# Two attentions in one kernel: raw loads parked in the second one's weight place, and the first 512 rows' five tiles grown together

## The chip, the core and the metric

One core of one Trainium2 chip runs the kernel. The metric is the device time of one execution in microseconds (us); less is better. TensorE does the matmuls, VectorE and ScalarE elementwise work, GpSimd elementwise work in the on-chip buffers and its own queue of transfers; SyncE (SP) and ScalarE issue transfers (DMAs) from their queues in order, and an issue that waits holds what is behind it.

## What is computed

Two independent attentions over 2048 rows of width 576, with 32 heads of 18. The outputs are put side by side.

```python
def _A_ref(x, wq, wk, wv, wo):                 # one key and one value head for all 32 query heads
    q = (x @ wq).reshape(B, S, H, Dh).transpose(0, 2, 1, 3)
    k, v = x @ wk, x @ wv
    p = softmax(einsum("bhqd,bkd->bhqk", q, k) * Dh ** -0.5)
    return merge_heads(einsum("bhqk,bkd->bhqd", p, v)) @ wo

def _B_ref(x, wq, wk, wv, wo, beta):           # 4 segments of 512 rows, causal inside a segment
    q, k, v = heads(x @ wq), heads(x @ wk), heads(x @ wv)
    g = sigmoid(beta)
    for s in range(4):
        a_dot = softmax(q_s @ k_s.T * scale + mask) @ v_s
        a_mem = (phi(q_s) @ M) / (phi(q_s) @ z + 1e-6)
        o_s = g * a_mem + (1 - g) * a_dot
        M, z = M + phi(k_s).T @ v_s, z + phi(k_s).sum()
    return o @ wo
```

## The kernel before

The kernel has two stages. The first, the projections, runs to about 330 us; the second, the attention itself, takes the rest, in an order written out by hand. Only the first is touched. In the first stage a scheduler decides, when the program is built, in which order each engine's instructions stand; it takes them up as soon as their buffers are free, so a load written late in the text may stand early in a queue. The times in this document come from the chip.

Every product in single precision is made of exact parts: an operand is split into a high part and a low part (`xh`, `xl` for x; `wAh`, `wAl` for A's weights; `wBh`, `wBl` for B's), and three products are summed. The contraction over 576 runs in five slices `k`: four of 128 rows, and a last one of 64 rows which stands twice, so that one slice holds both parts. A tile of the projection is thus 4 x 3 + 2 = 14 matmuls of 512 columns (`proj`).

The projection of A goes over four groups of 512 rows (`c`), each with five tiles `t` in the order 4, 0, 1, 2, 3. Tile 4 carries the last four query heads, the key and the value. Each tile has a bank of the matmul memory, `pj` (four buffers; another bank, `mm`, is used later for small things). Emptying a tile takes: for tile 4 a maximum on VectorE (`km`), a copy of the value on ScalarE (`vT`), four transposes on TensorE and a copy on VectorE (`VA`); for each tile its magnitude on ScalarE (`AQ`), the high part on ScalarE and the low part on VectorE (`split2`, tile `qp`, two buffers), and a store of `qp` to memory from SP's queue (`store_parts`). The bank is free when the low part is done; `qp` is free when its store has landed.

`load_xk` loads one slice of x from SP's queue into `xr` (three buffers), casts it to `xh` on VectorE and subtracts on VectorE to get `xl`; `next_x` takes the two buffers of `xh` and `xl` for a group of rows, and the slices of the next group are written between the tiles of the present one. `load_wk` loads one slice of weights from SP's queue into `wr` (two buffers), casts it on ScalarE and subtracts: on VectorE for A's weights, on GpSimd for B's. B's weights come in three column ranges: 504 to 1152 beside A's third group, 1152 to 1728 beside A's fourth, and 0 to 504 beside the first tiles of B's first segment. The masks and constants (`hmask`, `bmask`, `sel`, `zmask`, `selx`, `sely`, `ones_d`) and seven small transfers of beta into `gt` are issued from ScalarE's queue; an exponential on ScalarE and three steps on VectorE make the gate of `gt`.

Behind A's tiles stand a small matmul with `sel` (L285), 20 matmuls for A's shift (L294), and then B's segments: five tiles of keys (L361 on), `phi` of them (`ph_e` on ScalarE, `kf` on VectorE), transposes of `kf` (L343), `values` (L401), and four tiles of queries. B's x uses the same `xr`.

At the very start TensorE runs nine matmuls on zeros (L161).

## Time and profile before

| | |
|---|---|
| median of three runs | 1467.9 us (1465.7 to 1470.0) |
| the profiled execution | 1467.1 us, its span 1465.4 us |
| granted TensorE clock, mean over the span | 0.993 |
| busy, share of the span | TensorE 98%, ScalarE 81%, VectorE 71%, GpSimd 15% |
| transfers | 166.3 MB, 113 GB/s in the mean |

The span is the time from the first to the last instruction of the profiled execution; some 1.7 us lie around it. In the rows of the profile a group's line gives the line of the kernel, engine, operation, output and inputs, shapes and count, then busy us and the mean in ns, then the idle time before these instructions and what ended it. In a timeline the two first numbers are the start and the duration in us, and a bracket holds the idle time before and its releaser. PE is TensorE, PEld its weight loads, DVE VectorE, ACT ScalarE, POOL GpSimd, SPq and ACTq the queues of transfers. The matmuls are pipelined, so one that shows 0.39 us can be followed by the next after 0.23.

### The profile page before, as it was taken

The page shows a single profiled execution, that of the slowest core. Times are in us where ns is not written, and L with a number is a line of the kernel's source. Part 1 is how long each engine was busy: PE and PEld are TensorE (multiplying, and loading weights), DVE is VectorE, ACT ScalarE, POOL GpSimd, SP SyncE. Part 2 cuts the span into 40 slices and gives each one's busy share as a digit, 9 for nine tenths or more (in the row PEclk, how much of TensorE's full clock was granted, in tenths as well). Part 3 has the DMA queues.
Part 4 walks back from the last instruction along what each step waited for, and adds up shares of the span by engine and source line. Part 5 has one row for each costly group of instructions (what it writes and reads, how often), then busy time and mean ns, then how long its engine had stood idle before and what let it go on. Part 6 is the DMA issues. An engine that isn't in the chain of part 4 may idle for free.

```text
span 1465.4 us, 40738 instructions
## 1 busy us (share of the span) xinstructions
PE 1429.3 (98%) x17540; PEld 843.1 (58%) x17540; DVE 1033.6 (71%) x1217; ACT 1193.1 (81%) x1424; POOL 224.7 (15%) x291
## 2 busy tenths in 40 slices
PE   7988999998999999999999999999999999999998
PEld 5767878774554555555555555555555555555565
DVE  5465745646767778887778787787778887787761
ACT  3334333348999999999999999999999999999970
POOL 1031000000232211603110150131112400100001
PEclk9999999999999999999999999999999999999999
DMA  6675653455745243533222251233104221210022
GB/s 176 221 247 190 190 165 112 149 167 159 210 124 180 80 139 127 152 116 98 83 74 73 97 168 56 72 111 100 50 31 130 79 72 36 67 42 17 17 80 79
DMA packets 88243, 166.31 MB, mean 113 GB/s; under 512 B 12737, under 2 KB 21499, under 8 KB 87883
## 3 DMA queue, kind: packets, MB, share of 16 engines
q1 hardware_dynamic: 81510, 157.82, 34.4%
q10 hardware_dynamic: 6549, 5.85, 1.3%
q8 instruction: 138, 2.26, 0.6%
q14 instruction: 46, 0.38, 0.1%
HBM read 96.15 MB, written 67.49 MB: 112 GB/s over the span
## 4 chain that ended last, share of the span: by engine, by line
PE 63%; ACT 8%; DMA 3%; issue 2%; DVE 1%; POOL 0%; SPq 0%; DVEq 0%; POOLq 0%; ACTq 0%
PE O L818 29%; PE E L770 18%; PE F L667 11%; ACT P L788 8%; PE E L779 3%; PE E L667 1%; PE O L667 1%; DMA sm<-oB 1%; DMA stA<-qA 0%; DMA rB<-sm 0%; DMA stB<-kB 0%; DVE W L785 0%; DMA stB<-qB 0%; DMA out<-osb 0%; DMA rb<-rB 0%
## 5 line engine op out<-in xcount | busy, mean ns | idle before, releaser
L788 ACT ACTIVATE P<-E 128x1024 f32<-128x1024 f32 (+1 forms) x800 | 788.7, 1078 | 14.3 <-PE E L770 10.4
L785 DVE COPY W<-E 128x1024 f32<-128x1024 f32 (+1 forms) x384 | 461.2, 1201 | 185.5 <-PE E L770 122.5
L818 PE MATMUL O<-P,VA 128*32 128x256 f32 x7936 | 509.8, 380 | 0.0
L788 ACT ACTIVATE P<-W 128x1024 f32<-128x1024 f32 (+1 forms) x384 | 434.6, 1132 | 0.9 <-DVE W L785 0.8
L818 PEld LDWEIGHTS O<-P,VA 128*32 128x32 f32 x7936 | 262.7, 110 | 146.5 <-issue 10.1
L770 PE MATMUL E<-stA,kstA 56*128 56x512 f32 x1920 | 330.2, 439 | 2.2 <-ACT P L788 1.3
L770 PEld LDWEIGHTS E<-stA,kstA 56*128 56x128 f32 x1920 | 154.6, 184 | 180.1 <-ACT P L788 117.9
L793 POOL TENSOR_SCALAR_AFFINE_SELECT P<-P 128x256 f32<-128x256 f32 (+1 forms) x192 | 94.1, 493 | 446.1 <-ACT P L788 412.2
L667 PE MATMUL F<-woB,o 126*32 126x192 f32 (+1 forms) x1920 | 127.6, 338 | 0.0
L654 POOL TENSOR_TENSOR o<-o,rb 126x512 f32<-126x512 f32 (+1 forms) x40 | 56.7, 1424 | 435.1 <-DMA o<-oA 269.5
L750 DVE SCALAR_TENSOR_TENSOR q<-q,PD 128x1024 f32<-128x1024 f32 x96 | 120.9, 1260 | 0.0
L111 ACT CAST qp<-pj 126x512 fp32r<-126x512 f32 (+1 forms) x56 | 32.6, 584 | 66.7 <-DVE kmB L365 48.4
L818 PE MATMUL O<-P,vseg 128*32 128x256 f32 (+2 forms) x1536 | 82.1, 345 | 1.3 <-POOL P L793 1.2
L667 PEld LDWEIGHTS F<-woB,o 126*32 126x32 f32 (+1 forms) x1920 | 38.2, 108 | 70.9 <-issue 61.5
L667 PE MATMUL F<-woA,o 126*32 126x192 f32 (+1 forms) x1240 | 77.7, 338 | 0.6 <-DVE osb L692 0.6
L112 DVE TENSOR_TENSOR qp<-pj,qp 126x512 fp32r<-126x512 f32 (+1 forms) x56 | 38.3, 687 | 55.9 <-ACT qp L111 55.7
L209 PE MATMUL pj<-xh,wBh 128*126 128x512 f32 x180 | 73.4, 411 | 2.6 <-DVE xh L181 2.6
L827 DVE COPY oe<-O 128x512 f32<-128x512 f32 x64 | 44.3, 692 | 41.3 <-PE O L818 40.8
L209 PE MATMUL pj<-xh,wBl 128*126 128x512 f32 x180 | 71.6, 398 | 0.0
L779 PE MATMUL E<-stB 56*128 56x256 f32 (+3 forms) x512 | 62.2, 348 | 2.5 <-ACT P L788 2.0
L818 PEld LDWEIGHTS O<-P,vseg 128*32 128x32 f32 x1536 | 48.3, 109 | 26.8 <-POOL P L793 2.5
L209 PE MATMUL pj<-xl,wBh 128*126 128x512 f32 x144 | 59.4, 412 | 0.0
(134 smaller groups left out, 1373.7 us busy)
## 6 DMA issues: line engine op xcount, KB each, us to landing
stB<-kB SPq DMA_DIRECT2D x96, 144.0 KB
stB<-qB SPq DMA_DIRECT2D x32, 288.0 KB
stA<-qA SPq DMA_DIRECT2D x30, 288.0 KB
oA<-oe SPq DMA_DIRECT2D x32, 256.0 KB
oB<-oe SPq DMA_DIRECT2D x32, 256.0 KB
qA<-qp SPq DMA_DIRECT2D x16, 504.0 KB
kB<-qp SPq DMA_DIRECT2D x16, 504.0 KB
qB<-qp SPq DMA_DIRECT2D x16, 504.0 KB
```

Of the source, the lines that this page charges most:

```text
L112: nc.vector.tensor_tensor(qp[:R, 1, :n], src, qp[:R, 0, :n].bitcast(F32), op=ALU.subtract)
L209: nc.tensor.matmul(dst, w[:, c0 : c0 + M], x, start=i == 0, stop=i == len(ops) - 1)
L654: steps = [lambda: v.tensor_tensor(o, o, rb, op=ALU.mult)]
L667: nc.tensor.matmul(dst[32 * j : 32 * j + 32], parts[ab, c][: RT[t], t, r0 : r0 + 32], wo[ab][: RT[t], t, c0 : c0 + n], start=start, stop=stop,
L750: steps.append(lambda a=a: v.scalar_tensor_tensor(q, q, a, p, op0=ALU.add, op1=ALU.mult))
L770: nc.tensor.matmul(e[:, j], kstA[rows, 128 * kt : 128 * kt + 128], st[rows, h, :], start=True, stop=True)
L779: nc.tensor.matmul(e[:, j, c0 : c0 + 512 - 128 * k], st[rows, 4 + h, ks], st[rows, h, 128 * k :], start=True, stop=True)
L785: nc.vector.tensor_copy(src[:, :, :n], e[:, :, :n])
L788: nc.scalar.activation(p[:, :, :n], src[:, :, :n], AF.Exp, scale=SCALE)
L793: nc.gpsimd.affine_select(diag, diag, pattern=[[0, 2], [0, m], [1, 128]], base=0, channel_multiplier=-1, compare_op=ALU.is_ge, fill=0.0)
L818: nc.tensor.matmul(o[32 * j : 32 * j + 32, q0 : q0 + n], v, p[:, j % 2, p0 : p0 + n], start=m == hf == 0, stop=last and hf == 1,)
L827: nc.vector.tensor_copy(osb, o)
```

## The change

Three things are changed, all in the first stage.

- The raw data of the start get a place of their own. `wBl` and `wBh`, which B's weights fill only from A's third group on, are first taken as raw tiles (`raw`): A's whole weight and the x of the first and second group lie in the first, the x of the third group in the second. The weights and the second group's x are loaded from SP's queue and the first group's x from ScalarE's, with no `xr` or `wr` in between; the third group's x is loaded beside the first group's tiles. The tiles `wBl` and `wBh` are taken anew at A's third group, so B's weights wait until the raw data in them have been split. The first group's x is cast to `xh` on ScalarE instead of VectorE.
- The five tiles of the first group grow together: the loop runs over the slices `k` outside and the tiles inside, 15 matmuls a slice (10 for the last), with five banks held at once, the fifth being `mm`. They are emptied after that as before.
- The seven constants and the seven transfers of beta are issued from GpSimd's queue. B's weight slices for the first two column ranges alternate between the two `wr` buffers of one pool and two more of another.

```diff
+        raw = [pw.tile([128, 5, 3 * D], F32, name=n) for n in ("wBl", "wBh")]
+        XRAW = [(raw[0], CA), (raw[0], CA + C), (raw[1], 0)]
+
+        def load_part(dst, w, c0, n, k, queue):
+            for rows, src in halves(k):
+                queue.dma_start(dst[rows], w[src, c0 : c0 + n])
+
+        def xraw(c, k):
+            tile_, c0 = XRAW[c]
+            return tile_[:, k, c0 : c0 + C]
+
         def load_xk(xh, xl, xT, c, k):
-            t0 = c * C
-            xr = px.tile([128, C], F32, name="xr", bufs=3)
-            for rows, src in halves(k):
-                nc.sync.dma_start(xr[rows], xT[src, t0 : t0 + C])
-            nc.vector.tensor_copy(xh[:, k], xr)
+            if xT is a_xT and c < 3:
+                xr = xraw(c, k)
+            else:
+                xr = px.tile([128, C], F32, name="xr", bufs=3)
+                load_part(xr, xT, c * C, C, k, nc.sync)
+            (nc.scalar.copy if xT is a_xT and c == 0 else nc.vector.tensor_copy)(xh[:, k], xr)
...
-        def load_wk(wh, wl, w, c0, n, k, first):
...
+        def split_w(wh, wl, wr, c0, n, k, engine):
+            nc.scalar.copy(wh[:, k, c0 : c0 + n], wr)
+            engine.tensor_tensor(wl[:, k, c0 : c0 + n], wr, wh[:, k, c0 : c0 + n].bitcast(F32), op=ALU.subtract)
+
+        def load_wk(wh, wl, w, c0, n, k, pool=pt):
+            wr = pool.tile([128, 648], F32, name="wr", bufs=2)[:, :n]
+            load_part(wr, w, c0, n, k, nc.sync)
+            split_w(wh, wl, wr, c0, n, k, nc.gpsimd)
...
+        TILES = (4, 0, 1, 2, 3)
...
             if c == 0:
+                for k in range(5):
+                    load_part(raw[0][:, k, :CA], a_w, 0, CA, k, nc.sync)
+                    load_part(xraw(0, k), a_xT, 0, C, k, nc.scalar)
+                for k in range(5):
+                    load_part(xraw(1, k), a_xT, C, C, k, nc.sync)
+                nc.sync.dma_start(ident, ident_d)
                 xh, xl, fillx = next_x(a_xT, 0)
+                nx = next_x(a_xT, 1)
+                for t in TILES:
+                    ready[t] = ps.tile([128, C], F32, name="mm", bufs=1) if t == 3 else ps.tile([128, C], F32, name="pj", bufs=4)
                 for k in range(5):
-                    load_wk(wAh, wAl, a_w, 0, CA, k, True)
                     fillx(k)
-                nc.sync.dma_start(ident, ident_d)
+                    split_w(wAh, wAl, raw[0][:, k, :CA], 0, CA, k, nc.vector)
+                    parts_ = [(wAh, xh), (wAh, xl), (wAl, xh)] if k < 4 else [(wAh, xh), (wAl, xh)]
+                    for i, (w, x) in enumerate(parts_):
+                        for t in TILES:
+                            M = 114 if t == 4 else 126
+                            nc.tensor.matmul(
+                                ready[t][:M],
+                                w[:, k, 126 * t : 126 * t + M],
+                                x[:, k],
+                                start=k == 0 and i == 0,
+                                stop=k == 4 and i == 1,
+                            )
+                for k in range(5):
+                    nx[2](k)
             else:
                 xh, xl = nx[:2]
-            nx = next_x(a_xT, c + 1) if c < NCH - 1 else next_x(b_xT, 0)
+                nx = next_x(a_xT, c + 1) if c < NCH - 1 else next_x(b_xT, 0)
+                if c == 2:
+                    wBl, wBh = (pw.tile([128, 5, 3 * D], F32R, name=n) for n in ("wBl", "wBh"))
...
-                nx[2](t)
+                if c == 0:
+                    load_part(xraw(2, t), a_xT, 2 * C, C, t, nc.sync)
+                if c:
+                    nx[2](t)
 
                 if c == 2:
-                    load_wk(wBh, wBl, b_w, 504, 648, t, False)
+                    load_wk(wBh, wBl, b_w, 504, 648, t, p1 if t % 2 else pt)
                 if c == 3:
-                    load_wk(wBh, wBl, b_w, 2 * D, D, t, False)
+                    load_wk(wBh, wBl, b_w, 2 * D, D, t, p1 if t % 2 else pt)
...
-                nc.scalar.dma_start(hmask[:126], hmask_d)
...
+                nc.gpsimd.dma_start(hmask[:126], hmask_d)
...
-                    nc.scalar.dma_start(
+                    nc.gpsimd.dma_start(
                         gt[: RT[t], t : t + 1], b_beta[lo : lo + nh][:, None].to_broadcast([nh, DH])[:, :, None]
                     )
```

35 lines of the change are left out of this document (15 added, 20 removed).

## The prediction

> **What bounds the kernel now.** I read the page first, then busy time by stretch, then what TensorE waited for, then the timeline of the first 120 us.
>
> ```profile
> PE 1429.3 (98%) x17540; PEld 843.1 (58%) x17540; DVE 1033.6 (71%) x1217; ACT 1193.1 (81%) x1424; POOL 224.7 (15%) x291
> ```
>
> TensorE is the bound; what matters is where the missing 2% lies. I cut the projections at the first real matmul (6.46 us), at the first matmul of A's second, third and fourth 512 rows, at the end of A's tiles (91.99), at B's first `values` matmul (119.36), and at 330. Columns: length, then busy time of TensorE, its weight loads, VectorE, ScalarE and GpSimd, then granted clock, DMA share, GB/s.
>
> ```profile
> 0.00:6.46 6.46, 4.02 (x10) 1.19 (x10) 1.43 (x6) 1.99 (x2) 0.44 (x6) 1.00 0.69 193
> 6.46:34.75 28.29, 22.35 (x75) 16.50 (x75) 17.84 (x30) 8.22 (x14) 4.00 (x2) 0.88 0.63 175
> 34.75:51.66 16.91, 16.91 (x76) 13.17 (x74) 9.72 (x18) 6.76 (x12) 0.00 (x0) 1.00 0.55 179
> 51.66:70.79 19.13, 17.11 (x75) 12.98 (x74) 8.93 (x17) 6.88 (x12) 0.00 (x0) 1.00 0.74 232
> 70.79:91.99 21.20, 18.86 (x76) 14.21 (x75) 12.38 (x17) 8.11 (x14) 8.43 (x5) 0.92 0.73 229
> 91.99:119.36 27.37, 20.93 (x101) 14.98 (x100) 21.37 (x40) 9.09 (x16) 7.73 (x7) 0.94 0.76 252
> 119.36:330.00 210.64, 209.59 (x1162) 167.28 (x1161) 112.34 (x245) 78.45 (x165) 4.80 (x6) 1.00 0.49 161
> ```
>
> The second 512 rows are the yardstick: 70 projection matmuls and a few transposes in 16.9 us without a gap, about 0.23 us a matmul, 3.25 us a tile of 14. The same work takes 28.3, 19.1 and 21.2 us in the other three, and B's first five tiles lose over 6 us. From 119 us TensorE is busy 99.5%, so whatever is won before arrives at the end, unless the attention stage waits for something else:
>
> ```profile
> PE pj L209 <- DVE xh L181: 5.5, 4, 2.1
> ...
> PE tr L343 <- DVE kf L316: 4.6, 2, 3.8
> ...
> PE pj L209 <- DVE xh L185: 4.1, 1, 4.1
> ```
> ```profile
> PE E L770 <- ACT P L788: 3.0, 13, 0.6
> PE E L770 <- SPq L505: 2.5, 1, 2.5
> ```
>
> The first group (all before 130 us) is splits of x that came late; the second, the longest from 130 us to the end, is small and internal to its stage. So the change can touch some 20 us of gaps and half-clock time, no more.
>
> **Part 1: the start, later.** In the built order ScalarE's queue now issues x's six transfers, the fifth after x's first has landed and the sixth after x's second, and only then the table load and the first casts (x, then weights).
>
> ```profile
> 0.81 0.65 ACTq L258 DMA_DIRECT2D hmask<-hmask_c  x1
> ...
> 4.40 1.28 ACT L197 ACT_TABLE_LOAD   x1 [4.40 <-DMA hmask<-hmask_c]
> 5.54 0.43 DVE L181 CAST xh<-xr 128x512 fp32r<-128x512 f32 x1 [4.01 <-DMA xr<-a_xT]
> 5.70 0.71 ACT L197 CAST wAh<-wr 128x618 fp32r<-128x618 f32 x1
> ...
> 6.46 0.77 PE L209 MATMUL pj<-xh,wAh 128*114 128x512 f32 x1 [0.91 <-ACT wAh L197]
> ...
> 10.44 1.29 PE L209 MATMUL pj<-xh,wAh 128*114 128x512 f32 x4
> ```
> ```profile
> 2.00:6.00 4.00, 3.55 (x9) 0.99 (x7) 0.43 (x1) 1.59 (x2) 0.00 (x0) 1.00 0.95 276
> ...
> 13.00:17.00 4.00, 4.00 (x18) 3.13 (x18) 1.61 (x2) 0.75 (x2) 0.00 (x0) 1.00 0.26 19
> ```
>
> At 276 GB/s from 2 us, two slices of weights and x (2 x 565 KB) plus some constants land near 6.7; issue 0.35, table 1.28, two casts 0.6 + 0.71: first matmul near 9.8, 3.3 later than now (8.9 to 10.5 by how many constants go between). Behind it nothing starves: a slice of k is 15 matmuls, 3.5 us, and its data (565 KB) take 2 us. Now the queues fall idle at 13 to 17 us (19 GB/s) while the last slice waits for a buffer; that ends. The slow first matmuls stay: nine stand between 6.46 and 10.44, 0.44 each against 0.23, 1.9 us lost; after a longer idle time I take 2.4 (1.7 to 3.4). The 70 matmuls then end at 9.8 + 16.3 + 2.4 = **28.5** (27 to 30); now the first rows end at 34.75.
>
> **Part 2: five tiles end at once.** Now the fifth tile runs while the other four are emptied. After the change the next rows find every buffer full.
>
> ```profile
> L183 DVE TENSOR_TENSOR xl<-xr,xh 128x512 fp32r<-128x512 f32 x24 | 21.2, 892 | 0.4
> L112 DVE TENSOR_TENSOR qp<-pj,qp 126x512 fp32r<-126x512 f32 (+1 forms) x25 | 16.9, 686 | 12.9 <-ACT qp L111 12.8
> L181 DVE CAST xh<-xr 128x512 fp32r<-128x512 f32 x30 | 16.5, 557 | 12.6 <-DMA xr<-a_xT 8.9 <-DMA xr<-b_xT 3.6
> ...
> L238 DVE TENSOR_REDUCE km<-pj 114x1 f32<-114x512 f32 x4 | 2.8, 691 | 7.0 <-PE pj L209 7.0
> ```
> ```profile
> L111 ACT CAST qp<-pj 126x512 fp32r<-126x512 f32 x21 | 12.3, 586 | 19.4 <-DMA qA<-qp 15.0 <-DVE kmB L365 3.2 <-DMA kA<-qp 0.8
> ...
> L245 ACT ACTIVATE AQ<-pj 126x512 bf16<-126x512 f32 x16 | 9.6, 599 | 15.5 <-PE pj L209 15.5
> ...
> L198 POOL TENSOR_TENSOR wBl<-wr,wBh 128x648 fp32r<-128x648 f32 x5 | 9.0, 1807 | 73.5 <-ACT wBh L197 73.5
> ...
> L197 ACT CAST wBh<-wr 128x648 fp32r<-128x648 f32 x5 | 3.7, 736 | 7.5 <-DMA wr<-b_w 7.5
> ```
>
> I walk the built queues in time after 28.5, by these means (casts of x 0.42 undisturbed, 0.43 at 5.54 above). VectorE's maximum of tile 4 ends 0.2 before it; the next in its queue, two casts and a subtraction of the third rows' x, waited for the first rows' xh and end at 1.6; ScalarE has by then done two AQ and vT, so VA is through at 1.9, one xl at 2.55, tile 4's low part at 3.25. TensorE stands that long. VectorE goes on with another low part, casts and three xl, the last at 7.2. ScalarE's first cast of B's weights, which goes into the place of raw x, has to wait for that; behind it stand a second cast (8.7), vT (9.3), AQ, a third cast (10.6), qp (11.15) and then VectorE's low part: the third tile of the second rows gets its buffer at 11.9, where TensorE would want it at 10.65: 1.25 lost. Further weights of B wait on buffers that GpSimd frees (about 2 us each, five in a row) and then on their transfer, with ScalarE's queue standing behind each:
>
> ```profile
> 50.70 0.33 SPq L116 DMA_DIRECT2D qA<-qp  x1
> ...
> 71.71 0.37 SPq L196 DMA_DIRECT2D wr<-b_w  x1
> ```
> ```profile
> 54.45 0.58 ACT L111 CAST qp<-pj 126x512 fp32r<-126x512 f32 x1 [2.00 <-DMA qA<-qp]
> ...
> 76.27 0.73 ACT L197 CAST wBh<-wr 128x648 fp32r<-128x648 f32 x1 [1.54 <-DMA wr<-b_w]
> ```
>
> A store takes 3.7 us to land, a load 4.5 in traffic; I take 3.5 to 4, the queues being emptier. GpSimd frees buffers at 9.95, 11.95 and so on to 17.95. The load issued at 12.4 lands at 16, its cast, AQ, two qp and the low part reach 19.15: TensorE wanted it at 18.4, 0.75 lost. The load issued at 18 lands at 21.6, two casts, qp and low part reach 24.35 against 22.4: 1.95. Then VectorE splits the fourth rows' x (3.3, the first cast slowed by GpSimd) ahead of the next low part, 29.2 against 27.65: 1.55. From there each tile finds its buffer, and the third rows end at 28.5 + 42.6, the fourth at 28.5 + 59.6 = **88.1**, against 91.99: 3.9 saved. The third rows' x and the fourth's are there long before (issued 40 and 15 us ahead), so the 2.0 of 51.66:70.79 and the gaps and half clock of 70.79:91.99 (4.3) are gone; 5.5 of new buffer waits, 3.25 of standing and 3.3 of later start eat most of what the first rows win.
>
> The half clock could come back:
>
> ```profile
> 29.84 0.50 PE L209 MATMUL pj<-xh,wAh 128*126 128x512 f32 x1 [1.39 <-DVE qp L112]
> ```
> ```profile
> 31.40:34.80 3.40, 3.40 (x10) 2.60 (x9) 3.40 (x2) 0.38 (x1) 3.35 (x2) 0.50 0.77 226
> ```
>
> This half-clock stretch (ten matmuls in 3.4 us) followed a gap of only 1.39 us behind four tiny transposes, and cost some 1.5. After the gap of 3.25 the same loss would lie under the wait for 11.9, and so is charged nothing; after the gap of 1.55 it would not, and I leave 1.5 in the range. The Trainium skill's "TensorE: Matmul & The Clock Gate", Part 1, has the clock halved after an idle window of about 3.4 us; by that none of the new gaps would cost anything, while this trace shows less idle time to be enough.
>
> **Part 3: B's first five tiles.** Now VectorE waits there for B's first x, which stood on the load queue behind weights waiting for GpSimd. After the change x's five slices are issued 15 to 30 us before their use, and two more weight buffers keep the queue moving. What is late next is kf: VectorE does fm and shift (3.3), then three key maxima, four cast-and-subtract pairs of the second segment's x and two subtractions, which end 16.3 us after the stretch's start; TensorE has 14.85 of work to there (four tiles 13, the 20 small matmuls 1.3, issue). Wait 1.45, one more tile and two transposes: 20.4 against 27.37, 7.0 saved. VectorE alone holds 21.37 us of work now, of which the last two x pairs go elsewhere, so less than 18.5 is impossible and 21.4 quite possible. The smaller wait for kf behind it (4.6 - 3.8 = 0.8) goes too: the later maxima and copies leave VectorE room by then.
>
> **Part 4: constants from GpSimd.** Fourteen small transfers leave ScalarE's queue. Nothing in this trace is issued by GpSimd's queue; the nearest rows:
>
> ```profile
> 8.23 4.06 ACTq L268 DMA_DIRECT2D gt<-b_beta  x5
> ```
>
> That is 0.81 each on ScalarE's queue, 11 us for fourteen; at the other end, one by one with hmask's issue-to-landing of 3.6 us (0.81 to 4.40), 50 us. I take 1.5, nearer the first as eight may be under way: ready near 24. The exponential of gt waits for all of them and stands in ScalarE's queue ahead of the first AQ (wanted at 27.8), so they cost nothing up to 1.9 us each, and one for one above.
>
> **Sum.** 3.9 + 7.0 + 0.8 = 11.7 off the profiled execution's 1467.1 (the span is 1465.4): **1455.4**; the three runs' median, 1467.9, is 0.8 above it.
>
> **Rivals.** *ScalarE starved by B's weights*: loads take 4.5, twice in the chain (+2), half clock after 1.55 (+1.5), and the fourth rows' tiles late too, so half of part 3's gain goes (+3.5): 1462.4. For it: 15 us of qp's idle time already ends on stores. Against: the queues run emptier. *VectorE is the bound in B's first tiles* (21.37 of 27.37 busy): its 21.4 us stand, and four casts and xl beside GpSimd go by their means (557, 892 ns) and not by 420 and 690, +1.4: the stretch takes 22.8, +2.4, and with a start of 30 +1.5: 1459.3. With the first rival on top nearly all is lost: 1466.3. *Constants late, slower*: at 3.6 us each gt is ready at 51, TensorE stands 23 us longer, 11.7 are won: 1478.7. It turns slower from 2.75 us each on. For it: VectorE splits x and weights at that very time, and the two engines disturb each other here (xl 892 ns in the mean, where the undisturbed subtraction of the same size takes 686). *Constants a little late*: at 2.1 us each, between the two rows, ready at 30.2, 2.4 too late: 1457.8. The Trainium skill's "DMA: Bandwidth & Descriptors", in "SWDGE vs HWDGE vs iDMA", says that GpSimd writes such transfers' descriptors into SBUF and that VectorE's two-port modes lock it out meanwhile, which ScalarE's and SP's transfers do not suffer; its "Anatomy of one DMA" gives 2.0 us plus bytes / 436e3 for one. An estimate from that page, one by one, is 0.8 + 28 + 0.9 = 29.7, 1.9 too late, 1457.3; no run here shows such a transfer yet. *It does not load at once*: the order holds eight transfers in flight; that is in part 1 already.
>
> **How the numbers follow.** Forecast 0.60 (own range 1450.5 to 1459.5: start 27 to 30 is 1.5 either way, VectorE's 18.5 or 21.4 in part 3 is 1.9 less or 1.0 more, transfers 1 us quicker or slower on two waits 2); VectorE-bound 0.05; constants a little late 0.05; ScalarE starved 0.17, somewhat over half of it past the bound; nearly all lost 0.05; slower 0.08. The bound is 0.3%, 4.4 us, about what a measurement tells from no change when three runs spread 4.3. Faster 0.60 + 0.05 + 0.05 + 0.10 = 0.80, within 0.3% 0.07 + 0.05 = 0.12, slower 0.08. The range reaches past the starved case, 1450.5 to 1463.5; outside are all lost and slower, 0.13, and some tail.
>
> **What would show it.** First projection matmul at 9 to 10.5; its 70th by 30; then 2.5 to 4 us without projection; fourth rows' end at 86 to 91; first `values` matmul near 108 instead of 119.4. Wrong: gt's exponential later than 28, ScalarE idle on B's weights for over 6 us between 30 and 60, or VectorE without a gap from 88 to 110. If the stage after B's first segment no longer fills TensorE, the sum fails as a whole.

## The result, and the profile after

The changed kernel takes 1463.7 us in the median of 22 runs (1460.6 to 1466.9), the kernel before 1468.1 beside it (1462.5 to 1471.6): a ratio of 0.9973, 95% interval 0.9963 to 0.9983. That is 4 us faster, a little over a third of the 11.7 that were forecast, and just outside the range. The profiled execution took 1465.1 us (span 1463.4); executions of one kernel differ by several us, so below the profiles say where time goes and the medians say how much.

TensorE's busy time is that of before within a microsecond (first row, from the page); what changed is where it stands and at which clock. The busy time by stretch of the changed kernel, cut at the same events as before and once more at the end of the first rows' 70 matmuls: first projection matmul, that end, first matmul of the second, third and fourth rows, end of A's tiles, first `values` matmul:

```profile
PE 1428.4 (98%) x17540; PEld 845.3 (58%) x17540; DVE 1022.1 (70%) x1212; ACT 1197.1 (82%) x1429; POOL 233.2 (16%) x305
```
```profile
0.00:10.74 10.74, 4.02 (x9) 1.20 (x10) 1.18 (x6) 2.56 (x4) 7.01 (x18) 1.00 0.83 249
10.74:28.64 17.90, 17.86 (x70) 13.85 (x70) 12.33 (x25) 5.46 (x11) 1.68 (x3) 1.00 0.96 216
28.64:31.76 3.12, 0.42 (x4) 0.32 (x5) 3.03 (x7) 3.07 (x7) 0.00 (x0) 0.86 1.02 296
31.76:54.75 22.99, 20.29 (x74) 14.81 (x74) 7.87 (x15) 11.66 (x20) 12.04 (x8) 0.87 0.61 202
54.75:73.29 18.54, 18.52 (x75) 14.36 (x75) 9.69 (x18) 6.31 (x11) 0.00 (x0) 0.91 0.67 213
73.29:90.75 17.46, 16.88 (x75) 13.16 (x74) 9.54 (x19) 8.21 (x14) 3.07 (x2) 1.00 0.79 257
90.75:117.42 26.67, 21.80 (x101) 16.45 (x100) 21.25 (x38) 10.00 (x18) 7.06 (x6) 0.87 0.74 231
117.42:328.00 210.58, 210.58 (x1168) 168.06 (x1166) 109.94 (x243) 75.91 (x159) 1.05 (x3) 1.00 0.48 156
```

The first rows now end at 28.64 instead of 34.75, and the fourth rows have all but lost their gaps. But the second rows take 22.99 where they took 16.91, and B's first tiles 26.67, hardly less than the 27.37 of before. From the first `values` matmul to the end of the span it is 1346.0 us in both kernels.

The changed kernel's timeline of TensorE, the rows with the largest gaps, and the granted clock (third number from the end) behind three of them:

```profile
10.74 1.62 PE L255 MATMUL pj<-xh,wAh 128*114 128x512 f32 x3 [5.18 <-ACT wAh L207]
...
31.76 0.77 PE L222 MATMUL pj<-xh,wAh 128*114 128x512 f32 x1 [1.65 <-DVE qp L112]
...
54.75 0.77 PE L222 MATMUL pj<-xh,wAh 128*114 128x512 f32 x1 [2.41 <-DVE qp L112]
...
110.71 1.07 PE L386 MATMUL tr<-ident,kf 126*128 126x126 f32 x4 [3.38 <-issue]
```
```profile
31.76:37.80 6.04, 6.04 (x14) 4.47 (x15) 3.44 (x7) 1.79 (x3) 1.71 (x2) 0.51 0.69 248
54.75:58.20 3.45, 3.45 (x8) 2.62 (x9) 3.35 (x7) 0.59 (x1) 0.00 (x0) 0.51 0.57 190
...
111.00:116.00 5.00, 5.00 (x17) 4.11 (x16) 2.48 (x6) 1.59 (x3) 0.00 (x0) 0.50 0.82 239
```

Behind each of the three gaps TensorE ran at half clock for 3.5 to 6 us: the first tile of the second rows takes 6.04 for its 14 matmuls instead of 3.25.

### The profile page after: what moved, and what is told of

Its sections match the earlier page's. It is cut to its first block, busy times and chain, and to the rows that moved or that the text cites. A ratio compares the mean times of both kernels' runs of the same rounds, so it can differ in the third digit from the quotient of the medians.

```text
span 1463.4 us, 40751 instructions
## 1 busy us (share of the span) xinstructions
PE 1428.4 (98%) x17540; PEld 845.3 (58%) x17540; DVE 1022.1 (70%) x1212; ACT 1197.1 (82%) x1429; POOL 233.2 (16%) x305
## 4 chain that ended last, share of the span: by engine, by line
PE 63%; ACT 8%; DMA 3%; issue 2%; SPq 0%; DVE 0%; POOL 0%; ACTq 0%; DVEq 0%; POOLq 0%
PE O L861 29%; PE E L813 19%; PE F L710 11%; ACT P L831 8%; PE E L822 3%; PE E L710 1%; DMA rB<-sm 1%; DMA sm<-oB 1%; DMA stB<-shB 1%; PE O L710 1%; DMA stA<-qA 0%; DMA rA<-sm 0%; DMA out<-osb 0%; SPq L686 0%; DVE oe L870 0%
## 5 line engine op out<-in xcount | busy, mean ns | idle before, releaser
L697 POOL TENSOR_TENSOR o<-o,rb 126x512 f32<-126x512 f32 (+1 forms) x40 | 60.8, 1524 | 438.1 <-DMA o<-oA 266.4
```

The lines of the kernel that those rows point to most:

```text
L697: steps = [lambda: v.tensor_tensor(o, o, rb, op=ALU.mult)]
```

## The experiments

The theory after the result had two parts. In A, the five tiles that end together cost a standing, and the half clock behind it is a loss of its own. In B, whatever A wins comes back as a wait for `kf`, since VectorE's queue stands there on the second segment's x. The rivals: the later start, ScalarE held by B's weights, the constants, and VectorE or the load queue simply full. This table has what the runs gave, but for three told further down. The first four columns of numbers are from the profiled execution, in us; the ratio is to runs of the kernel before beside them, whose medians were 1466.8 to 1468.1. All but bcst are edits of the changed kernel. One execution stands behind these four columns: for s1, cst, bcst, xg and s1_xg it was the fastest of the kernel's runs, for tm_xg and tm_s1xg the slowest, so a difference of a few us between two rows can also be that of two executions. From the first `values` to the end of the span it takes 1343 to 1349 us in all kernels of the table but tm_xq (1351.7).

| kernel | A's tiles end | wait for `kf` | first `values` | span | median | ratio to before, interval |
|---|---|---|---|---|---|---|
| before | 91.99 | 3.8 | 119.36 | 1465.4 | 1468.1 | 1 |
| changed | 90.75 | 3.4 | 117.42 | 1463.4 | 1463.7 | 0.9973, 0.9963 to 0.9983 |
| clk | 88.40 | 6.9 | 118.66 | 1461.8 | 1464.8 | 0.9994, 0.9977 to 1.0011 |
| stag2 | 81.62 | 7.3 | 114.55 | 1460.9 | 1461.3 | 0.9949, 0.9930 to 0.9967 |
| tm | 82.80 | 5.9 | 113.26 | 1458.8 | 1459.9 | 0.9945, 0.9926 to 0.9964 |
| s1 | 87.05 | 2.8 | 111.70 | 1457.4 | 1462.4 | 0.9971, 0.9958 to 0.9984 |
| wgp | 94.35 | 7.0 | 123.69 | 1468.9 | 1470.1 | 1.0019, 1.0001 to 1.0036 |
| cst | 94.49 | 3.8 | 120.90 | 1464.1 | 1470.6 | 1.0021, 1.0008 to 1.0033 |
| bcst (before, constants alone) | 87.05 | 4.0 | 115.81 | 1462.2 | 1466.2 | 0.9991, 0.9978 to 1.0004 |
| xg | 88.56 | 2.1 | 110.21 | 1456.7 | 1461.1 | 0.9956, 0.9941 to 0.9972 |
| tm_xq | 82.18 | 6.1 | 113.94 | 1465.6 | 1466.1 | 0.9988, 0.9974 to 1.0002 |
| tm_xg | 83.95 | 3.2 | 112.35 | 1457.6 | 1459.4 | 0.9949, 0.9935 to 0.9962 |
| stag2_xg | 81.24 | 3.6 | 112.49 | 1458.6 | 1460.3 | 0.9960, 0.9946 to 0.9974 |
| tm_s1xg | 87.11 | 3.1 | 114.22 | 1461.7 | 1461.3 | 0.9948, 0.9931 to 0.9965 |
| tm_xgp3 | 83.58 | 1.4 | 109.40 | 1458.2 | 1461.3 | 0.9959, 0.9945 to 0.9974 |
| s1_xg | 86.92 | 1.5 | 108.28 | 1455.2 | 1462.3 | 0.9968, 0.9951 to 0.9985 |
| wpt | 94.56 | 3.7 | 119.01 | 1467.6 | 1466.5 | 0.9997, 0.9986 to 1.0008 |

### The half clock, and the tiles that end together

```diff
 (clk, on the changed kernel: behind the 70 matmuls)
+                pz = ps.tile([128, C], F32, name="nd", bufs=2)
+                for _ in range(14):
+                    nc.tensor.matmul(pz, xh[:, 4].bitcast(BF)[:, 0:128], xh[:, 4].bitcast(BF)[:, 0:C], start=True, stop=True)
```

> The changed kernel with 14 bf16 matmuls of 128x512 (some 3 us, into a spare bank) put behind the 70 matmuls of the first rows, so that TensorE works while it waits for the first free bank. Nothing else is changed. Theory (the half clock behind the standing of 3.1 us is a loss of its own, and was wrongly charged at nothing): the first tile of the second rows runs at 0.23 a matmul instead of 0.43, its ScalarE copy and the transposes come 2.8 us earlier, the second rows take 20 to 20.5 us instead of 22.99, A's tiles end near 88 instead of 90.75. Rival (as predicted, the loss lies under the wait for the third bank): the waits for banks behind it grow by what the first tile wins, second rows 22.5 or more, A's end within 0.7 of 90.75.

The stretches of this kernel, the first being the extra matmuls and the transposes, the second matmuls of the second rows:

```profile
28.00:31.60 3.60, 3.60 (x18) 1.69 (x17) 1.21 (x2) 3.28 (x7) 0.00 (x0) 1.00 0.97 323
31.60:37.00 5.40, 5.40 (x27) 4.02 (x25) 5.34 (x12) 1.39 (x3) 0.00 (x0) 1.00 0.75 247
```
```profile
111.56 1.07 PE L389 MATMUL tr<-ident,kf 126*128 126x126 f32 x4 [6.88 <-issue]
```

The clock stays up there and A's tiles end at 88.40, 2.35 earlier: the half clock was a loss, not hidden. It comes back once in this kernel, behind a gap of 1.88 (row in the last section). In the end nothing is won, since the wait for `kf` doubles to 6.88. This was the first sign that A's end doesn't set the result.

```diff
 (stag2: the order of the first rows' matmuls)
+                    todo += [(k, i, w, x) for i, (w, x) in enumerate(parts_)]
+                    if k < 2 or k == 4:
+                        by_tile = [(t, p) for t in TILES for p in todo] if k == 4 else [(t, p) for p in todo for t in TILES]
...
 (tm: no growing together; raw transfers and constants as changed)
-                    pj = ready[t]
...
+                pj = ps.tile([128, C], F32, name="pj", bufs=4)
+                proj(pj[:M], wAh, wAl, xh, xl, 126 * t, M)
```

> The changed kernel with slices 0 and 1 of k for all five tiles in turn, and slices 2 to 4 tile by tile, so that the five tiles end 1.85 us apart instead of within 1.2 us. Theory (the five tiles ending together is what costs): first rows end at 28.5 to 29.5, the standing of 3.1 us falls to under 1 us, no half clock behind it, A's tiles end at 85 to 87. Rival (ScalarE, held by the casts of B's weights and by stores, is what keeps the second rows slow): the standing goes, but waits for banks in the second rows take its place and A's tiles end at 89 or later.

> The changed kernel with only the growing together undone: raw transfers and constants as changed, but each tile's 14 matmuls in a row, in a bank of its own as before. Theory: the first tile waits for the last slice of k, which lands at 17 to 20, the first rows end at 31 to 33 (3 to 4 later than changed), there is no standing of 3 us behind them and no half clock (5.9 together), so A's tiles end at 88 to 90, as early as changed or earlier. Rival (growing together is the gain of the change): A's tiles end at 93 or later.

Both beat their theories for A's end: its tiles end 9 and 8 us earlier than in the changed kernel, and of that 2.4 and 3.8 us reach the median. With the tiles one after the other (kernel tm) TensorE is busy for 70.58 of the 72.05 us from its first projection matmul to A's end, at full clock:

```profile
10.75:82.80 72.05, 70.58 (x296) 54.55 (x297) 41.37 (x75) 32.92 (x58) 13.10 (x10) 1.00 0.77 225
```

So what pays is the rest of the change, raw transfers, constants and buffers together, and growing together, the most laborious part, costs some 4 us of it (the intervals of the two ratios just touch, at 0.9964 and 0.9963). No run has the raw transfers alone.

### The start, ScalarE and the constants

```diff
 (s1)
-                    load_part(xraw(0, k), a_xT, 0, C, k, nc.scalar)
+                    load_part(xraw(0, k), a_xT, 0, C, k, nc.scalar if k < 3 else nc.sync)
 (wgp)
-            nc.scalar.copy(wh[:, k, c0 : c0 + n], wr)
+            (nc.gpsimd.tensor_copy if wh is not wAh else nc.scalar.copy)(wh[:, k, c0 : c0 + n], wr)
 (cst, and the same line the other way round in the kernel before: bcst)
-                nc.gpsimd.dma_start(hmask[:126], hmask_d)
+                nc.scalar.dma_start(hmask[:126], hmask_d)
...
```

> The changed kernel with x's slices 3 and 4 of the first rows issued by SP, between the slices of weights, instead of by ScalarE, which then issues three transfers and has no wait for a landed one ahead of its table load. Theory: first projection matmul at 7 to 8.5 instead of 10.74, first rows end at 26 to 27, and A's tiles end 2 to 3 us earlier, 88 to 89. Rival (the transfers bound the first rows, or what follows waits for casts and stores that don't come earlier): first matmul earlier, first rows' end within 1 us of 28.64.

The first matmul comes at 6.65 and A's tiles end at 87.05, 3.7 earlier; the interval of this kernel's ratio and that of the changed one nearly coincide. The late start is real, and taking it away wins nothing that these runs can tell. Most of it is lost again at once: of the 4.1 us won at the first matmul 0.7 are left when the second rows start (31.07 for 31.76). The gate's exponential holds ScalarE's queue until 20.76, 5.86 of it waiting for beta, with x's last cast behind it; VectorE then splits the second rows' x first and takes the maximum `km` at 27.35, and `vT` waits for that. The earlier end of A arises in the second rows, 20.41 long instead of 22.99, with a wait of 0.90 instead of 2.41 behind them.

> The changed kernel with the casts of B's weights (15, 0.7 each on ScalarE) on GpSimd, which makes their low parts already; ScalarE's queue then never stands on them. Theory (a third of A's loss is ScalarE waiting on B's weights, which stood ahead of vT and qp in the second rows): the second rows take 21 or less instead of 22.99, the third rows have no standing of 2.41 at their start, A's tiles end at 87 to 88.5. Rival (the half clock and the stores of qp do it): second rows above 22, A's end within 1 us of 90.75. For B's first tiles: the weights come later (two operations of some 1.4 to 2 us in a row on GpSimd for each slice), so values may be no earlier than 117.

Neither theory nor rival fits as a whole. With the casts off ScalarE the second rows still take 25.3 us (32.71 to 58.05), with gaps of 1.88 and 3.07 on low parts, as the rival had it, but A's tiles end at 94.35. That ScalarE starves on B's weights is not shown; what GpSimd does instead makes other things late. Two casts of x on VectorE take 2.38 beside it (55.01), ahead of the low part that ends the second of these gaps, and B's key maxima wait for its last split:

```profile
106.72 1.29 DVE L408 TENSOR_REDUCE kmB<-pj 126x1 f32<-126x512 f32 x2 [4.63 <-POOL wBl L208]
```

> The changed kernel with one part undone: the fourteen constants go from ScalarE's queue again, where they stand behind the last cast of the first rows' weights and ahead of gt's exponential and the first AQ. At 0.65 to 0.81 us each they take 9 to 11 us of ScalarE's queue from some 19 us on. Theory (the move to GpSimd's queue is needed for the rest and costs nothing itself): gt's exponential at 30 to 35 instead of 19.42, vT and the first AQ behind it, second rows start 3 to 6 us later than 31.76, A's end 93 to 96. Rival (GpSimd's transfers slow VectorE or come late): A's end at 90 or earlier, and x and weights split faster than changed in the first 28 us.

> The kernel before with only the constants moved to GpSimd's queue. Theory (on their own they win little: ScalarE's queue holds 14 issues of 0.65 to 0.81 there, but the first rows are bound by x's buffers and the load queue): first matmul 1 to 2 us earlier than 6.46, A's end within 1.5 us of 91.99, the whole within 2 us of before. Rival (the constants are the change's gain: undone in the changed kernel they cost 7 us): 4 us or more faster than before.

The constants on ScalarE's queue again (kernel cst) make the gate's exponential 13.7 us later than in the changed kernel, where all fourteen are issued by 12.42:

```profile
11.13 1.29 POOL L315 DMA_DIRECT2D gt<-b_beta  x2
```
```profile
19.42 0.21 ACT L318 ACTIVATE gt<-gt 128x7 f32<-128x7 f32 x1 [3.17 <-DMA gt<-b_beta]
```
```profile
33.16 0.21 ACT L318 ACTIVATE gt<-gt 128x7 f32<-128x7 f32 x1 [18.58 <-DMA xr<-a_xT]
```

(The last row is of the kernel cst; the transfer in its bracket is the one that landed last by the profile.) The theory for cst held: with that move undone the change is 3 us slower than before, so it is needed. The first rows' `vT` stands behind the exponential, and TensorE waits 6.98 us for it. Alone in the kernel before the move ends A 4.9 us earlier, against the theory, and wins 1.3 us by the ratio, as the theory had it, which can't be told from nothing.

### What sets kf in B's first tiles

VectorE, ScalarE, GpSimd and SP's queue of the changed kernel between A's end and `kf`:

```profile
91.40 2.89 DVE L332 TENSOR_SCALAR kbdA<-hmask,kAp 126x32 bf16<-126x32 f32 x5
...
96.80 1.65 DVE L124 TENSOR_TENSOR shp<-sht,shp 128x512 fp32r<-128x512 f32 x1
...
101.75 0.43 DVE L194 CAST xh<-xr 128x512 fp32r<-128x512 f32 x1 [2.43 <-DMA xr<-b_xT]
...
105.22 1.65 DVE L196 TENSOR_TENSOR xl<-xr,xh 128x512 fp32r<-128x512 f32 x1
...
107.72 1.28 DVE L112 TENSOR_TENSOR qp<-pj,qp 126x512 fp32r<-126x512 f32 x2
...
109.81 0.69 DVE L359 SCALAR_TENSOR_TENSOR kf<-pj,ph_e 126x512 f32<-126x512 f32 x1
```
```profile
108.52 0.60 ACT L356 ACTIVATE ph_e<-pj 126x512 f32<-126x512 f32 x1 [3.83 <-DVE qp L112]
```
```profile
91.49 2.47 POOL L208 TENSOR_TENSOR wBl<-wr,wBh 128x504 fp32r<-128x504 f32 x2 [3.80 <-ACT wBh L207]
...
96.50 1.40 POOL L208 TENSOR_TENSOR wBl<-wr,wBh 128x504 fp32r<-128x504 f32 x1 [1.03 <-ACT wBh L207]
...
104.77 1.55 POOL L208 TENSOR_TENSOR wBl<-wr,wBh 128x504 fp32r<-128x504 f32 x1 [3.67 <-DMA shA<-shp]
```
```profile
95.32 0.36 SPq L182 DMA_DIRECT2D xr<-b_xT  x1
97.93 1.17 SPq L182 DMA_DIRECT2D wr<-b_w  x2
99.15 4.11 SPq L182 DMA_DIRECT2D xr<-b_xT  x3
```

VectorE stands 2.43 us on the second segment's x, which no matmul needs before the first segment is through; the key maxima and the two low parts stand behind it, ScalarE's `ph_e` behind these, `kf` behind that. One slice of this x was issued at 95.32, the next three from 99.15 on, behind two slices of weights.

```diff
 (xg: the second segment's x split by GpSimd; its five casts and five subtractions leave VectorE)
+            eng = nc.gpsimd if xT is b_xT and c == 1 else nc.vector
 (tm_xq: split as changed, transferred by GpSimd's queue; tiles one after the other)
+                load_part(xr, xT, c * C, C, k, nc.gpsimd if xT is b_xT and c == 1 else nc.sync)
```

> The changed kernel with one thing else: the second segment's x (five casts, five subtractions, the first of which stand on VectorE between B's first key maxima and their low parts) is split by GpSimd instead of VectorE. Theory (what is won before B comes back as a wait for kf, because VectorE's queue stands there on x that is not yet needed): low parts, the exponential and kf come 3 us or more earlier, TensorE's 3.4 us ahead of kf's transposes and the half clock behind go, the first values matmul comes at 112 to 114 instead of 117.42, and the whole is 3 to 5 us faster than changed. Rival (VectorE is simply full there, or GpSimd's splits slow it and make B's weights late): the wait for kf or a wait for weights stays above 2.5 us and values come at 116 or later.

```profile
88.56:110.21 21.65, 18.94 (x101) 14.40 (x100) 14.83 (x27) 8.31 (x15) 13.66 (x15) 1.00 0.79 246
```

In this kernel the stretch from A's end to the first `values` takes 21.65 instead of 26.67, at full clock, with 14.83 us of VectorE instead of 21.25. The median gains 2.6, somewhat less than the theory's 3 to 5, and the intervals of the two kernels overlap at their ends. The stretch is shorter with this edit in each pair of the table that differs by it alone: 21.36 for 24.65 (s1_xg and s1), 28.40 for 30.46 (tm_xg and tm), 31.25 for 32.93 (stag2_xg and stag2). It takes from VectorE both the wait for x and the work on it, so the shares of the two are not told apart.

> The first rows' tiles one after the other, and the second segment's x still split by VectorE, but transferred by GpSimd's queue instead of SP's, where it stands behind weights that wait for buffers. Theory (VectorE stood on x because the transfers were issued late, not because of the splits themselves): VectorE's waits for x between B's first maxima (4.2 us in one piece) go, wait for kf 2 to 4 instead of 5.9, values at 109 to 112, 1456 to 1459. Rival (GpSimd's queue issues them no earlier, as its own splits of weights stand ahead): wait for kf above 5, values at 113 or later.

The rival's numbers came: the wait for `kf` stays at 6.11, and the kernel is 6 us slower than with SP's queue (kernel tm). But its reason didn't: GpSimd issues the first of these slices at 86.03, where SP issued it at 93.01, and VectorE's wait of 4.19 for it (in tm) is 1.36 here. Instead VectorE stands 3.83, until 94.45, on two casts, of which at least one is the first segment's, as TensorE takes it up at 94.93. And of the 6 us only 0.7 lie ahead of the first `values` (113.94 for 113.26); the rest lies behind it (1351.7 for 1345.5 to the end). So this run doesn't settle whether the late x or the work of splitting it on VectorE is what makes `kf` late.

> The changed kernel with two edits together: the first rows' tiles one after the other (A's end came at 82.9 with that alone, but 5.9 us of waiting for kf gave most of it back) and the second segment's x split by GpSimd (which alone took the wait for kf from 3.4 to 2.1). Theory (the two losses are separate, A's rows and VectorE's queue standing on x): A's end 82 to 84, wait for kf under 2.5 us, values at 105 to 109, 1453 to 1457. Rival (a third thing, GpSimd's own queue with B's last weights behind x, takes over when A ends earlier): values at 111 or later, 1458 or more.

> Slices 0 and 1 for all five tiles, 2 to 4 tile by tile (A's end 81.7 with that alone, 8.4 us of waiting for kf), and the second segment's x split by GpSimd. Theory: A's end 81 to 83, wait for kf under 3 us, values at 105 to 109, 1453 to 1457. Rival: as A ends earlier than B's weights and shA's stores allow, kf waits for these instead, values at 111 or later, 1458 or more.

> Three edits on the changed kernel together: first rows' tiles one after the other (no growing together), x's slices 3 and 4 issued by SP, and the second segment's x split by GpSimd. Theory (each takes away a wait of its own): first matmul at 7, A's tiles end at 80 to 82, wait for kf under 2 us, values at 104 to 108, in all 1450 to 1455. Rival (the wait for kf is set by something that doesn't move with A's end, such as B's weights or stores): values at 111 or later, 1458 or more.

None is additive. A's tiles end at 81 to 84 in the first two, yet the first `values` come at 112.4, and the medians stay within 1 us of those without the split on GpSimd. In the third the first tile stands on the last slice of x. Its cast stands in ScalarE's queue right behind the gate's exponential, and that waits for beta, which GpSimd's queue loads:

```profile
21.32 0.77 PE L223 MATMUL pj<-xh,wAh 128*114 128x512 f32 x1 [4.66 <-DVE xh L199]
```
```profile
19.83 0.21 ACT L303 ACTIVATE gt<-gt 128x7 f32<-128x7 f32 x1 [5.07 <-DMA gt<-b_beta]
```

For tm_xg the trace names what comes next, the key maximum waiting for GpSimd:

```profile
97.17 1.29 DVE L393 TENSOR_REDUCE kmB<-pj 126x1 f32<-126x512 f32 x2 [1.78 <-DMA shA<-shp]
```
```profile
95.71 1.43 POOL L209 TENSOR_TENSOR wBl<-wr,wBh 128x576 fp32r<-128x576 f32 x1 [3.78 <-ACT wBh L208]
```

The small tile of the maxima takes over memory of A, in which the change put two weight buffers; the maximum starts as GpSimd's last split from there ends (97.14). The bracket names a store of `shA` that landed last, but in tm_xgp3 below the same maximum starts at 94.82, before the last of these stores is issued (94.9), so it doesn't need them. Five runs asked whether that, or the load queue, is the rest.

```diff
 (wpt: both weight groups; tm_xgp3: the second line only, with tm and xg)
-                    load_wk(wBh, wBl, b_w, 504, 648, t, p1 if t % 2 else pt)
+                    load_wk(wBh, wBl, b_w, 504, 648, t)
-                    load_wk(wBh, wBl, b_w, 2 * D, D, t, p1 if t % 2 else pt)
+                    load_wk(wBh, wBl, b_w, 2 * D, D, t)
 (wq, tm_wq, tm_wqxg: B's weights transferred by GpSimd's queue)
-            load_part(wr, w, c0, n, k, nc.sync)
+            load_part(wr, w, c0, n, k, nc.gpsimd)
```

> The changed kernel with one part undone: all of B's weights use the two buffers they had before, none lies in A's memory (which the key maxima's small tile takes over after A, and so waits for GpSimd's last split from there). Theory (the two buffers keep the load queue moving, the wait they bring for the maxima is hidden while A ends at 90): the splits of B's second weights end later, x stands behind them on the load queue again, values at 118 to 121, 1464 to 1467. Rival (the maxima's wait for A's memory is what makes kf late): values at 115 or earlier and 1461 or less.

The theory's times came: without the two buffers the kernel is 2.8 us slower than changed (1466.5), and the intervals don't meet. Its reason is not what the trace shows: the loss lies in A, whose tiles end 3.8 later (94.56), with TensorE waiting 1.89 at 42.73 and 2.42 at 80.28; B's first tiles take 24.45 instead of 26.67, and VectorE's wait for the second segment's x is 1.79 instead of 2.43. In the changed kernel itself the maxima's wait is hidden: the first maximum starts at 98.37, as VectorE's operation before it ends.

> The changed kernel with B's weights transferred by GpSimd's queue, which also frees their buffers, instead of SP's, where x, the stores and the next weights stand behind each wait for a buffer. Theory (SP's queue standing on weights' buffers makes the second segment's x late, and that x stands ahead of the low parts on VectorE): x lands before VectorE wants it, wait for kf under 2.5 us instead of 3.4, values at 111 to 114, 1458 to 1461. Rival (GpSimd's transfers are slow beside its own splits, so B's weights are later than now): waits for wB in B's first tiles, values at 117 or later.

> The first rows' tiles one after the other, and B's weights transferred by GpSimd's queue. A ends at 82 to 84 here, and the question is what holds B's first tiles to values at 112 to 114 even so. Theory (the load queue, with B's weights and the second segment's x behind stores and buffers): wait for kf under 3 us, values at 106 to 110, 1454 to 1457. Rival (VectorE's work between A's end and kf, some 21 us, is the floor): values at 111 or later, 1458 or more.

> The same with the second segment's x split by GpSimd as well, which takes 3 to 5 us of work from VectorE ahead of kf. Theory (queue and VectorE's work both): values at 103 to 107, 1451 to 1455. Rival (a floor that neither touches, such as the stores or the exponential on ScalarE): values at 110 or later.

All three are 11 to 16 us slower than before (1479.1, 1477.9, 1482.8; ratios 1.0089, 1.0078, 1.0110, with intervals of 1.0075 to 1.0103, 1.0063 to 1.0092 and 1.0094 to 1.0126), and A's tiles end past 107. ScalarE now takes up B's weights early and stands on their transfers, with `qp` behind; from the timelines of ScalarE and VectorE of tm_wq:

```profile
60.59 0.67 ACT L207 CAST wBh<-wr 128x576 fp32r<-128x576 f32 x1 [5.17 <-DMA wr<-b_w]
```
```profile
62.84 0.69 DVE L112 TENSOR_TENSOR qp<-pj,qp 126x512 fp32r<-126x512 f32 x1 [11.11 <-ACT qp L111]
```

So they don't answer the question they were made for (with A ending so late, the wait for `kf` is 1.5 to 1.6 in all three); they show what the forecast's rival of a starved ScalarE looks like when it does happen.

> First rows' tiles one after the other, the second segment's x split by GpSimd, and B's second group of weights (576 columns) in the two old buffers, so that no tile of B has to wait for GpSimd's last split out of A's memory (VectorE stood 1.78 on that at 97.17 when A ended at 84). Theory (that wait and what stands behind it is the last piece of the late kf): first maximum of B at 94 to 96, wait for kf 1 to 2.5 us, values at 108 to 111, 1456 to 1458.5. Rival (fewer buffers cost as much on the load queue as the wait): values at 112 or later, 1459 or more.

> The changed kernel, growing together kept, with x's slices 3 and 4 of the first rows issued by SP (alone: first matmul 6.65, A's end 87.0) and the second segment's x split by GpSimd (alone: wait for kf 2.1). Theory (start and VectorE's queue are separate losses): A's end 86 to 88, wait for kf under 2.5, values at 107 to 110, 1457 to 1459.5. Rival (B's first tiles can't come earlier than 110, whenever A ends): values at 110 to 113, 1460 or more.

In tm_xgp3 the first maximum waits for TensorE alone, and `kf`'s transposes start 3.7 us earlier than in tm_xg:

```profile
94.82 0.69 DVE L393 TENSOR_REDUCE kmB<-pj 126x1 f32<-126x512 f32 x1 [1.35 <-PE pj L223]
```
```profile
101.73 0.62 PE L371 MATMUL tr<-ident,kf 126*128 126x126 f32 x4 [1.43 <-issue]
```

The theory's milestone held (109.40), its time didn't: 1461.3. From there to the end it is 1348.8 instead of the changed kernel's 1346.0, with further waits for `kf` of 1.88 and 1.68, the second of them behind the first `values`. s1_xg brings the first `values` to 108.28, the earliest of all, in an execution that was its fastest (1457.1); its twelve runs spread to 1468.6, and the median is no better than that of s1. Why the same program's executions differ by 11 us is left open; many of the waits above end on a transfer that lands, and a single profile can't average these.

Best in the median are tm_xg and tm, 1459.4 and 1459.9, 0.5% under the kernel before and some 4 us under the changed one; the two can't be told apart, nor, by the ratios, from tm_s1xg and stag2.

## Why the prediction was wrong

The profiled execution came out at 1465.1 against 1455.4. The missing 9.7 us are A's end 2.65 later than the sum had it (90.75 for 88.1), B's first tiles 6.27 longer (26.67 for 20.4), and the 0.8 for a smaller wait behind. That wait did go (TensorE has no idle time from 117.42 to 328), but the way from the first `values` to the end is as long as before: in the attention stage, for one, TensorE waits 2.7 for a `P` from GpSimd, where it was 1.2.

**Part 1 held.** First rows' end 28.64 for 28.5. The first matmul came 0.94 late, because ScalarE's queue held longer on x's transfers than I had taken; the slow first matmuls were fewer.

```profile
0.83 7.31 ACTq L182 DMA_DIRECT2D wBl<-a_xT  x6
8.17 1.28 ACT L194 ACT_TABLE_LOAD   x1 [8.17 <-DMA wBl<-a_xT]
```

**Part 2 failed at one step**: the half clock "would lie under the wait" for the third bank "and so is charged nothing". The standing was right (3.12 for 3.25), and so was the wait of ScalarE for the last split of raw x. But the wait for the bank isn't fixed in time. ScalarE's queue has `vT` of the second rows ahead of the remaining `qp` of the first, and `vT` waits for the very tile that runs at half clock:

```profile
35.27 1.36 ACT L207 CAST wBh<-wr 128x648 fp32r<-128x648 f32 x2 [3.08 <-DVE xl L196]
38.74 0.58 ACT L280 COPY vT<-pj 18x512 f32<-18x512 f32 x1 [2.10 <-DVE km L278]
...
40.46 0.58 ACT L111 CAST qp<-pj 126x512 fp32r<-126x512 f32 x1
```

With the clock kept up there, and nothing else changed, A's tiles end at 88.40: the forecast's 88.1 but for 0.3. That it comes so near is in part luck. Of the 5.5 charged for waits for banks the changed kernel has 2.6, and the largest, 2.41 at 54.75, is not for B's weights: the low part there waits for a `qp` that waited for its store.

```profile
53.39 0.59 ACT L111 CAST qp<-pj 126x512 fp32r<-126x512 f32 x1 [2.47 <-DMA qA<-qp]
```

The half clock, charged at nothing, costs 2.8 in the second rows (6.04 for 3.25) and 1.6 in the third (3.45 for eight matmuls). The rule of the Trainium skill that was weighed there ("TensorE: Matmul & The Clock Gate", Part 1: half clock after an idle window of about 3.4 us) would have charged nothing either; a gap of 2.41 us (at 54.75) was enough here.

**Part 3 failed, and it is the larger share.** I had named the right wait (`kf`) and sized it at 1.45, by VectorE's work alone. Measured: TensorE reached `kf`'s transposes 1.73 us later (at 107.33, 16.58 us behind A's end, for 14.85), mostly since it had to wait for `kbdA` twice, 1.49 in all; then 3.38 of waiting; and 6.71 instead of 4.1 from there to the first `values`, with the clock halved behind that very wait. That is 1.73 + 1.93 + 2.61 = 6.27. Two things were left out of the sum. The split of the second segment's x waits for its transfer (2.43), though the part argued only about the first segment's. And GpSimd's splits of B's weights hold VectorE's operations: `kbdA` 2.89 where it took 0.82 before (row below), two subtractions 1.65 each for 0.69, 4.0 us in all. They fell into this stretch before as well (7.73 us of GpSimd's time, now 7.06) and held other operations, casts above all; what is new is that they meet `kbdA`, for which TensorE waits. Taking the second segment's splits off VectorE gave 21.65 for the stretch, in an execution that was its kernel's fastest; so the named wait was the right one, and its term was mis-sized. The share of GpSimd is read from one trace, and no run tests it alone.

```profile
92.50 0.82 DVE L289 TENSOR_SCALAR kbdA<-hmask,kAp 126x32 bf16<-126x32 f32 x5
...
96.19 1.29 DVE L123 CAST shp<-sht 128x512 fp32r<-128x512 f32 x1
```

**Part 4 held**: constants ready at 19.4 (24 was forecast; by the working of its own rivals, 0.8 and fourteen times 1.5, it would have been 21.8) and no cost against before. They were issued in 0.53 to 0.75 us each with eight under way: the ninth, at 8.16, waited for the first to land. The one-by-one estimate from the Trainium skill's "DMA: Bandwidth & Descriptors", 29.7, is not what the trace shows.

**The rivals.** The time is nearest to "ScalarE starved" (1462.4), but not by its mechanism: between 30 and 60 ScalarE waited 3.1 us for the place of B's weights and 0.4 for the weights, not over 6. It waited 6.3 there for stores of `qp`, which this rival had named in its favour. VectorE had gaps between 88 and 110, and still `kf` was late: the rival "VectorE is the bound" was right in the place and, as I read the trace, wrong in the reason: from A's end to `kf` VectorE stands 2.43 on x and loses 4.0 beside GpSimd, more than the 3.38 that TensorE waits. No run shows order and interference apart from the sum of its work. Of the three signs that were to show the forecast wrong only that of VectorE came near what happened, and it asked for a full engine where a blocked one did the harm.

The deeper fault is in how the sum was made: it added a gain in A to a gain in B. The table shows that they are not separate. With A's end anywhere between 81.2 and 88.6, `kf`'s transposes start at 104 to 112, against 110.71 in the changed kernel; only in tm_xgp3, with the splits moved and the maxima's place free, they start at 101.73.

## What to carry to other kernels

When a loss is charged at nothing because a wait covers it, ask whether what is waited for stands, in some queue, behind the very work that gets slower; if so it moves along, and nothing is covered. Gains of two stages in a row must not be added: take the new end of the first, then walk the queues of the second from there, transfers of data not yet needed included, since in an order fixed ahead they stand in front of what is needed. And a change of several parts wants its parts priced apart: here the raw loads, with the constants out of ScalarE's way, won 8 us by the ratio (kernel tm), and growing the tiles together gave about half of it back.

## What the hardware showed beside that

VectorE's subtractions of two on-chip tiles ended 0.55 us behind GpSimd's when the two met (98.45 behind 97.90; 106.87 behind 106.32), and took 1.65 instead of 0.69, while in xg two low parts, which read one operand from the matmul memory, took 1.28 together right across a cast and a subtraction of GpSimd:

```profile
102.70 1.28 DVE L112 TENSOR_TENSOR qp<-pj,qp 126x512 fp32r<-126x512 f32 x2
```
```profile
102.69 0.61 POOL L195 CAST xh<-xr 128x512 fp32r<-128x512 f32 x1
103.38 1.28 POOL L197 TENSOR_TENSOR xl<-xr,xh 128x512 fp32r<-128x512 f32 x1
```

It looks like a lock and not like sharing. The Trainium skill's "SBUF — State Buffer" says so in "SBUF: two separate sides": the port pair that VectorE and GpSimd have in common is held for a whole instruction, and the other one blocks fully; the traces here agree.

The half clock came after gaps of 1.88 (kernel clk, first row below), 2.41, 3.12 (with four tiny transposes in it) and 3.38 us, and lasted some 3 to 6; 14 bf16 matmuls that compute nothing kept the clock at 1.00 through the place of the 3.12. The length of the gap alone doesn't decide: behind gaps of 2.02 (second row, kernel before) and 2.07 (at 103.81 there) the clock stayed at 1.00.

```profile
49.10:52.30 3.20, 3.20 (x9) 2.51 (x8) 0.67 (x1) 0.00 (x0) 0.34 (x1) 0.51 0.69 228
```
```profile
56.65:58.50 1.85, 1.85 (x8) 1.39 (x9) 0.67 (x1) 0.46 (x1) 0.00 (x0) 1.00 0.89 290
```
